# Lambda times alpha1 as one row, spread by one product; lambda itself broadcast by a load

## The chip, the cores and the metric

The kernel runs on one core of a Trainium2 chip. The metric is the device time of one execution in microseconds (us). The core has five engines that the profile names: PE (matrix products; PEld are its weight loads, which overlap PE), DVE (vector work), ACT (activations and copies), POOL (GpSimd) and SP (it issues transfers). Transfers run on 16 DMA engines that all queues share. In this kernel SP and ACT issue the plain ones (queues q1 and q10 of the profile) and POOL those that also change the type (q0).

## What is computed

Attention over keys and values that are averaged in groups of 8, for 8 batches of 8 heads, 576 positions and width 64; then, on the result x (8 x 576 x 512), a residual block that mixes positions and then channels:

```python
k_p = k.reshape(B, H, Sp, 8, D).mean(axis=3)
v_p = v.reshape(B, H, Sp, 8, D).mean(axis=3)
scores = scale * np.matmul(q, k_p.transpose(0, 1, 3, 2))
...
x = attn_out.transpose(0, 2, 1, 3).reshape(B, S, H * D)
...
a1 = alpha1 * x + beta1
tok = np.einsum('ts,bsd->btd', w_tok, a1)
u = x + lam * tok
a2 = alpha2 * u + beta2
ch = np.maximum(a2 @ w_ch1, 0.0) @ w_ch2
return (u + lam * ch).astype(np.float32)
```

lam, alpha1, beta1, alpha2 and beta2 are vectors of 512. Since lam multiplies each column of tok, lam times alpha1 can be multiplied into x before the mixing, and lam times beta1 becomes one more row of the mixing product.

## The kernel before

Tokens are worked on in 9 blocks of 512. Each batch gives four chunks of 128 tokens (positions 0 to 511), and the last 64 positions of two batches make up a ninth. The program's order is written by hand: the tile framework places buffers and semaphores, but each engine runs its instructions in the order of the text. Batch 0 is written out line by line (L806 to L889). From there on a loop over the blocks (L943) gathers pieces of work with a place number each, sorts them by it and calls them (L1018). The first block's list also holds the attention of batch 1.

**Constants at the start.** The tile vecs (L205) has the vectors of the mixing in rows: row 0 of its partition dimension holds lam in slot 0, beta1 in slot 1, alpha1 in slot 2, and row 64 holds lam and beta1 once more. ACT issues the loads of lam (L210, called at L213), of two of the four pieces of the rem tile (L148; the last 64 positions of q and k for batch 0), of alpha1 (L218) and of beta2 (L222). SP issues the other two rem pieces, beta1 and alpha2 as rows of b2row. POOL issues q, k and v with a change of type. Meanwhile DVE fills constants; L276, L278 and L280 build the pooling matrices out of what POOL prepares, and come last before the program proper.

**Lambda and lambda times alpha1 on all 128 partitions.** The tile lam_bc holds lam in every partition, and lamal_bc holds lam times alpha1. spread_lam (L301) makes the first: a product of a row of ones (ones_row, 1 x 128) with the lam row, f32, into the PSUM tile ps_bc, and a copy by ACT (L305). spread_al1 (L307) makes the second in two halves of 256 columns: a product of ones with half of alpha1 (L311), then a product of that with lam_bc on DVE (L312).

**Batch 0.** In order: att_F transposes q (L402), cast_rem converts the rem pieces (L170), att_Frem transposes them (L426), spread_lam comes, then double_k and att_K form the pooled keys (L445, L451) and copy them to kpT (L461, one half on ACT, one on DVE), then spread_al1(0) and bias_row(0) (L284, lam times beta1, on DVE). The heads follow: att_S forms scores (L493, L496) and their exponentials (L498, ACT), first_V the pooled values (L472, L474, copy L477), att_AV the attention products (L556, L560) and the division (L562, L564, DVE). att_X (L578) and rest_X (L571) multiply x by lamal_bc into xs: heads 0 to 3 read columns 0 to 255, heads 4 to 7 the others. spread_al1(1) stands between the scores of head 6 and the attention product of head 5. load_al2 (L297) broadcasts alpha2 to all partitions by a load on SP, behind a DVE memset that sets the moment of its issue. keep_warm products on PE stand in gaps. setup_wtok transposes w_tok (L329). mix_T is the mixing product (L614) with the sum on DVE (L618) and, for batch 0, a product with al2_bc (L624).

**Who reads lam_bc later.** scale_w2 (L721) multiplies w2 by lam, from place 13.9 of the first block's list on; mlp_B (L688) multiplies the output of the first block by lam. After that w2 itself carries lam. setup_wtok_odd (place 8.3 of the first block) copies a part of wtT by two loads on SP (L347, L348), the second behind a DVE memset (L346). load_v32 loads batch 1's values on POOL's queue, and sum_v (L137) is the first to read them.

The lines that the change takes out or moves most:

```python
load_vector(0, moe_lam)
load_rem(0)
...
nc.scalar.dma_start(out=vecs[0:1, 2], in_=moe_alpha1.unsqueeze(0))
...
spread_lam()
double_k(0)
att_K(0, 0, None)
spread_al1(0)
...
att_S(0, 6)
spread_al1(1)
att_AV(0, 5)
```

Of the kernel before, what the change touches and what calls it, by code (L numbers as in the profile page):

```python
# [11 lines left out]
ALU = mybir.AluOpType  # L12
AX = mybir.AxisListType

P = 128
SPG = 72
DM = 512
# [6 lines left out]
def kernel(  # L24
# [18 lines left out]
    nc = tc.nc  # L43
# [8 lines left out]
    def gp(name):  # L52
        return psA.tile([P, 512], FP, tag="gp", name=name)
# [13 lines left out]
    def new_batch(b):  # L67
        st1[b] = {"qT": [None] * 2, "ET": [None] * H, "raw": [None] * 2, "q": [None] * 2,
                  "k": [None] * 2, "v": [None] * 2}
# [4 lines left out]
    def load_q_bf(b, u, behind=None):  # L74

        bf = work.tile([P, 4, 4, D], BF, tag="q_bf", bufs=4, name="q_bf")
        if behind is not None:
            behind.memset(bf[:, 0, 0, 0:1], 0.0)
        nc.gpsimd.dma_start(out=bf.rearrange("p h c d -> p h (c d)"), in_=rows(q, b, u))
        st1[b]["q"][u] = bf  # L80
# [60 lines left out]
    def load_rem(b, queue=nc.sync, behind=None):  # L141

        raw = work.tile([P, 2, 2, 2, D], FP, tag="rem_raw", bufs=2, name="rem_raw")
        if behind is not None:
            behind.memset(raw[:, :, :, 0, 0:1], 0.0)
        for i, src in enumerate((q, k)):
            for h in range(2):
                (nc.scalar if h and not b else queue).dma_start(  # L148
                    out=raw[:, i, h].rearrange("p c d -> p (c d)"),
                    in_=src[b, h::2, 512:576, :].rearrange("a (i c) d -> i a (c d)", c=2))  # L150
        st1[b]["rem_raw"] = raw
# [48 lines left out]
    lam_bc = const.tile([P, DM], FP, tag="lam_bc", name="lam_bc")  # L200
    lamal_bc = const.tile([P, DM], FP, tag="lamal_bc", name="lamal_bc")
# [3 lines left out]
    vecs = const.tile([65, 3, DM], FP, tag="vecs", name="vecs")  # L205
    ones_row = const.tile([1, P], FP, tag="ones_row", name="ones_row")
    nc.vector.memset(ones_row, 1.0)

    def load_vector(i, src, queue=nc.scalar):
        queue.dma_start(out=vecs[0:65:64, i], in_=src.unsqueeze(0).to_broadcast((2, DM)))  # L210

    new_batch(0)
    load_vector(0, moe_lam)  # L213
    load_rem(0)
    load_q_bf(0, 0)
    load_k16(0, 0)
    load_vector(1, moe_beta1, nc.sync)
    nc.scalar.dma_start(out=vecs[0:1, 2], in_=moe_alpha1.unsqueeze(0))  # L218
    start = const.tile([1, 2], FP, tag="start", name="start")
    nc.vector.memset(start, 0.0)  # L220
    nc.scalar.activation(out=start[:, 1:2], in_=start[:, 0:1], func=AF.Exp, bias=0.0, scale=1.0)
# [45 lines left out]
    for i in range(2):  # L267
# [5 lines left out]
    nc.vector.memset(pool_v[:, 64:], 0.0)  # L273
    nc.vector.memset(pool_vr, 0.0)
    nc.vector.memset(vr16, 0.0)
    nc.vector.tensor_scalar(out=pool_v[:, 0:64], in0=pool_main, scalar1=8.0, scalar2=None,  # L276
                            op0=ALU.mult)
    nc.vector.tensor_tensor(out=pool_vr[0:32, 64:72], in0=pool_v[0:32, 0:16:2],  # L278
                            in1=pool_v[0:32, 1:16:2], op=ALU.add)
    nc.vector.tensor_reduce(out=pool_rem, in_=pool_each, op=ALU.max, axis=AX.X)  # L280

    def bias_row(i):
        p0 = 64 - 64 * i
        nc.vector.tensor_tensor(out=xs_pool[i][p0:p0 + 1, 4, :], in0=vecs[p0:p0 + 1, 1],  # L284
                                in1=vecs[p0:p0 + 1, 0], op=ALU.mult)
# [12 lines left out]
        behind.memset(al2_bc[:, 0:1], 0.0)  # L298
        nc.sync.dma_start(out=al2_bc, in_=moe_alpha2.unsqueeze(0).to_broadcast((P, DM)))

    def spread_lam():  # L301

        ps = gp("ps_bc")
        nc.tensor.matmul(out=ps, lhsT=ones_row, rhs=vecs[0:1, 0])
        nc.scalar.copy(out=lam_bc, in_=ps)  # L305

    def spread_al1(half):  # L307

        ps = gp("ps_bc")[:, 0:256]
        cols = slice(256 * half, 256 * half + 256)  # L310
        nc.tensor.matmul(out=ps, lhsT=ones_row, rhs=vecs[0:1, 2, cols])  # L311
        nc.vector.tensor_tensor(out=lamal_bc[:, cols], in0=lam_bc[:, cols], in1=ps, op=ALU.mult)  # L312

    def setup_vectors():
        ps = gp("ps_vec")
# [19 lines left out]
    def setup_rowsum(tcx):  # L335

        trc = P if tcx < 4 else REM
        cols = slice(P * tcx, P * tcx + trc)
        ps = gp("ps_rs")
        for sc in range(5):  # L340
            nc.tensor.matmul(out=ps[:, 0:trc], lhsT=ones_bf if sc < 4 else ones_lo,
                             rhs=wtT[:, sc, cols], start=(sc == 0), stop=(sc == 4))
        nc.scalar.copy(out=wtT[64:65, 4, cols], in_=ps[64:65, 0:trc])
# [35 lines left out]
    def setup_bias(js):  # L379
        ps_bias = gp("ps_bias")  # L380
        for i, jc in enumerate(js):
            for cc in range(4):
                nc.tensor.matmul(out=ps_bias[0:P, i:i + 1], lhsT=w1_of(cc, jc),
                                 rhs=b2c_bf[:, cc:cc + 1], start=(cc == 0), stop=(cc == 3))
        nc.scalar.copy(out=bias_cols[:, js[0]:js[-1] + 1], in_=ps_bias[0:P, 0:len(js)])
# [45 lines left out]
    def double_k(u):  # L431

        nc.vector.tensor_copy(out=st1[0]["k"][u][:, :, 4], in_=st1[0]["k"][u][:, :, 0])
        if u == 0:
            cast_rem_k(nc.vector)

    def att_K(b, u, copy):

        st = st1[b]
        ps_kp = gp("ps_kp")  # L440
        kp = ps_kp[:, 0:4 * SPG].rearrange("p (h g) -> p h g", g=SPG)
        n, nr = (1, 1) if b else (4, 2)
        for h in range(4):
            for c in range(n):
                nc.tensor.matmul(  # L445
                    out=kp[:, h, 0:64],
                    lhsT=st["k"][u][:, h, c:c + 2].rearrange("p a d -> p (a d)"),
                    rhs=pool_main, start=(c == 0), stop=(c == n - 1))
        for hh in range(2):
            for c in range(nr):  # L450
                nc.tensor.matmul(  # L451
                    out=kp[:, hh:4:2, 64:72],
                    lhsT=st["rem"][1][:, hh, c:c + 2].rearrange("p a d -> p (a d)"),
                    rhs=pool_rem.rearrange("p (g u r) -> p u r g", r=2, u=2)[:, u],
                    start=(c == 0), stop=(c == nr - 1))
        if b:
            copy(out=kp_pool[u], in_=kp)
            return
        for a in range(2):
            rows = slice(64 * a, 64 * a + 64)  # L460
            (copy or (nc.scalar.copy, nc.vector.tensor_copy)[a])(  # L461
                out=kpT_pool[u][rows, a], in_=kp[rows])
# [138 lines left out]
    def keep_warm(count):  # L601

        ps = psB.tile([P, DM], FP, tag="ch", bufs=2, name="ps_warm")
        for _ in range(count):
            nc.tensor.matmul(out=ps, lhsT=warm[:, 0:P], rhs=warm)
# [211 lines left out]
    keep_warm(1)  # L817
    att_Frem(0, nc.scalar.copy)
    keep_warm(1)
    spread_lam()  # L820
    double_k(0)
    att_K(0, 0, None)
    spread_al1(0)
    bias_row(0)
    att_S(0, 0)
    att_S(0, 1)
# [18 lines left out]
    att_S(0, 5)  # L845
    att_AV(0, 4)
    att_S(0, 6)
    spread_al1(1)
    att_AV(0, 5)
    att_X(0, 4, 6, nc.gpsimd, False)  # L850
    att_S(0, 7)
# [91 lines left out]
    for n in range(NBLK):  # L943
        todo = []
# [26 lines left out]
        if n >= FIRST:  # L971
# [22 lines left out]
            else:  # L994
                for m in range(4):
                    todo.append((27.2 if m < 2 else 29.2, lambda m=m: store(n, m)))
        if n == 0:
            todo.append((6.2, lambda: setup_rowsum(4)))
            todo.append((8.3, setup_wtok_odd))
            for g in range(2, 4):  # L1000
                todo.append((4 * g - 0.8, lambda g=g: setup_bias(range(4 * g, 4 * g + 4))))
# [48 lines left out]
```

## Time and profile before

| | us |
|---|---|
| median of 3 runs | 333.59 |
| the three runs | 333.06, 333.59, 334.97 |
| the profiled execution | 333.62 |
| its span, first to last instruction | 331.9 |
| PE busy | 323.7 (98% of the span) |
| DVE busy | 233.6 (70%) |
| ACT busy | 175.7 (53%) |
| POOL busy | 95.2 (29%) |

The instructions that the change touches, from the trace's answers for their tiles:

| line | engine | what | count | ns each | start, us |
|---|---|---|---|---|---|
| L304 | PE | ones times lam, 1x512 f32 | 2 | 692 and 587 | 7.7, 8.2 |
| L305 | ACT | copy to lam_bc, 128x512 | 1 | 586 | 8.9 |
| L311 | PE | ones times half of alpha1, 1x256 f32 | 4 | 374 to 478 | 9.8 and 18.4 |
| L312 | DVE | lam_bc times that, 128x256 | 2 | 422 | 10.8, 19.2 |
| L299 | SP | issue of the alpha2 broadcast, 256 KB | 1 | 363 | 17.9 |

An f32 product stands as two passes in the trace, each with its own weight load. Times of matmuls are those of single instructions, which overlap their neighbours; the chain of waits gives what each adds to the path. In a view of the timeline a line reads: start, duration, engine, line of the program, operation, output from input, count, and in brackets how long the engine sat idle before it and what ended that. An engine's name with a q (ACTq, SPq) is the issue of a transfer, not the transfer. In a table by stretches the columns are the stretch, its length, busy time and count for PE, PEld, DVE, ACT and POOL, then the granted TensorE clock as a share of full speed, the mean number of DMA engines' share at work, and GB/s.

### The profile page before, as it was taken

What the parts mean: (1) busy time and instruction counts of PE and PEld (TensorE: products, weight loads), DVE (VectorE), ACT (ScalarE), POOL (GpSimd) and SP (SyncE); (2) the same over time, 40 slices, a digit from 0 to 9 for tenths busy, and PEclk for the clock granted to TensorE, in tenths of its full rate; (3) what the DMA queues carried; (4) which work ended last, traced back from release to release, by engine and by line L of the source; (5) the groups of instructions that cost most, each with busy time, mean ns of one, the idle gap of its engine ahead of it and who ended that gap; (6) DMA issues with size and microseconds to landing.
All of it is one profiled execution on the core that took longest, in us unless ns stands there. A gap on an engine that the chain in (4) does not pass through costs nothing.

```text
span 331.9 us, 6477 instructions
## 1 busy us (share of the span) xinstructions
PE 323.7 (98%) x2500; PEld 209.6 (63%) x2531; DVE 233.6 (70%) x485; ACT 175.7 (53%) x322; POOL 95.2 (29%) x110
## 2 busy tenths in 40 slices
PE   7999999999999999999999999999999999999995
PEld 3667864455544576656775677558755866586584
DVE  6674289989679969676967796877788783263263
ACT  3584989448422861388128812682268225703710
POOL 8669828401247011800280027102510200000000
PEclk9799999999999999999999999999999999999999
DMA  8999999966895992499449943996340044004003
GB/s 117 191 217 270 270 209 245 206 148 101 152 243 99 219 181 81 80 232 173 147 109 209 173 136 73 209 187 176 65 136 2 0 65 143 2 0 127 1 32 97
DMA packets 66472, 45.81 MB, mean 138 GB/s; under 512 B 34397, under 2 KB 57061, under 8 KB 66442
## 3 DMA queue, kind: packets, MB, share of 16 engines
q1 hardware_dynamic: 52092, 32.67, 43.3%
q0 software_dynamic: 13824, 12.40, 22.9%
q8 instruction: 20, 0.33, 0.4%
q10 hardware_dynamic: 526, 0.34, 0.4%
q14 instruction: 10, 0.08, 0.1%
HBM read 38.30 MB, written 9.44 MB: 144 GB/s over the span
## 4 chain that ended last, share of the span: by engine, by line
PE 94%; DMA 2%; DVE 1%; issue 1%; POOL 1%; ACT 0%; POOLq 0%
PE ps_h L662 38%; PE ps_w L785 26%; PE ps_tok L614 11%; PE ps_ch L682 8%; PE ps_av L556 3%; PE ps_s L513 2%; DMA k<-in_k_dram 2%; PE ps_kp L445 1%; PE ps_sc L493 1%; PE ps_r L520 1%; PE ps_av L560 1%; PE ps_v L472 0%; PE ps_w L329 0%; PE ps_q L402 0%; DVE u_sb L618 0%
## 5 line engine op out<-in xcount | busy, mean ns | idle before, releaser
L662 PE MATMUL ps_h<-u_fm,w 128*128 128x512 bf16 (+2 forms) x588 | 132.6, 368 | 1.3 <-DVE bias_cols L665 0.2
L669 ACT ACTIVATE H<-ps_h,bias_cols 128x512 bf16<-128x512 f32 x144 | 98.2, 688 | 56.5 <-PE ps_h L662 55.5
L662 PEld LDWEIGHTS <-w 128*128 128x128 bf16 x608 | 65.6, 114 | 49.9 <-issue 2.2
L785 PEld LDWEIGHTS <-H 128*128 128x128 bf16 x560 | 53.5, 98 | 10.8 <-DVE u_sb L803 1.2
L622 ACT CAST u_bf<-u_sb 128x512 bf16<-128x512 f32 x32 | 19.8, 618 | 69.9 <-issue 39.9
L785 PE MATMUL ps_w<-w_l,H 128*128 128x256 bf16 x448 | 53.6, 272 | 0.0
L803 DVE TENSOR_TENSOR u_sb<-u_sb,ps_w 128x512 f32<-128x512 f32 x54 | 36.3, 683 | 17.1 <-PE ps_w L785 17.1
L578 POOL TENSOR_TENSOR xs<-x_tm,lamal_bc 128x512 bf16<-128x512 f32 x12 | 15.9, 1328 | 108.7 <-DVE x_tm L564 108.5
L614 PE MATMUL ps_tok<-xs,wtT 128*128 128x512 bf16 (+3 forms) x194 | 44.6, 380 | 0.4
L618 DVE TENSOR_TENSOR u_sb<-x_tm,ps_tok 128x512 f32<-128x512 f32 (+1 forms) x40 | 27.4, 684 | 9.9 <-PE ps_tok L614 9.8
L564 DVE TENSOR_TENSOR x_tm<-ps_av,rec 128x320 f32<-128x320 f32 x64 | 31.5, 492 | 2.6
L542 ACT ACTIVATE ET<-ps_s 72x512 f16<-72x512 f32 x56 | 32.3, 592 | 0.0
L614 PEld LDWEIGHTS <-wtT 128*128 128x128 bf16 (+3 forms) x200 | 17.4, 100 | 16.0 <-issue 1.1
L562 DVE RECIPROCAL rec<-ps_av 128x5 f32<-128x5 f32 x64 | 12.2, 190 | 16.9 <-PE ps_av L560 16.7
L483 DVE TENSOR_TENSOR v_u<-v_u 72x1024 f32<-72x1024 f32 (+1 forms) x24 | 22.7, 948 | 0.2
L785 PE MATMUL ps_w<-w_t,h_s 128*128 128x256 bf16 x168 | 22.6, 272 | 0.0
L682 PEld LDWEIGHTS <-H 128*128 128x128 bf16 x128 | 11.9, 98 | 13.7 <-issue 0.4
L754 DVE TENSOR_TENSOR H<-H,H 128x1024 bf16<-128x1024 bf16 x14 | 9.7, 690 | 14.3 <-ACT H L669 14.2
L185 POOL TENSOR_TENSOR k_raw<-k_raw 128x512 f32<-128x512 f32 x14 | 18.8, 1341 | 0.9 <-PE ps_ch L682 0.7
L785 PEld LDWEIGHTS <-h_s 128*128 128x128 bf16 x168 | 16.4, 98 | 4.1
L187 POOL TENSOR_TENSOR k_bf<-k_raw 128x512 bf16<-128x512 f32 x14 | 18.5, 1319 | 1.1
L754 DVE TENSOR_TENSOR h_s<-H 128x1024 bf16<-128x1024 bf16 x21 | 14.4, 686 | 6.0 <-ACT H L669 5.8
(148 smaller groups left out, 367.6 us busy)
## 6 DMA issues: line engine op xcount, KB each, us to landing
out_dram<-u_sb SPq DMA_DIRECT2D x29, 256.0 KB
k_raw<-in_k_dram SPq DMA_DIRECT2D x12, 512.0 KB
v_u<-in_v_dram SPq DMA_DIRECT2D x12, 512.0 KB
q_bf<-in_q_dram POOLq DMA_DIRECT2D x16, 256.0 KB, 7.3
w<-in_moe_w_ch_dram POOLq DMA_DIRECT2D x6, 512.0 KB, 12.5
out_dram<-u_sb SPq DMA_DIRECT2D x11, 128.0 KB
w<-in_moe_w_ch_dram POOLq DMA_DIRECT2D x1, 1024.0 KB, 15.0
k_raw<-in_k_dram POOLq DMA_DIRECT2D x2, 512.0 KB, 16.8
```

What stands on the lines that cost most here:

```text
L483: nc.vector.tensor_tensor(out=out, in0=t[:, :, 0:width], in1=t[:, :, width:2 * width], op=ALU.add)
L542: nc.scalar.activation(out=o, in_=i, func=AF.Exp, bias=0.0, scale=0.125)
L564: nc.vector.tensor_tensor(out=x[:, 1 - odd:6 - odd, dd:dd + D], in0=av[:, :, 0:64], in1=rec.unsqueeze(2).to_broadcast((P, 5, D)), op=ALU.mult)
L614: nc.tensor.matmul(out=ps_tok[p0:p1], lhsT=wtT[0:kk, at, P * c:P * c + p1 - p0], rhs=xs_pool[i][0:kk, sc, :], start=(sc == 0), stop=(sc == 4))
L618: nc.vector.tensor_tensor(out=s["u"][p0:p1, :], in0=x[p0:p1, 1 + c if c < 4 else 5 - 5 * i, :], in1=ps_tok[p0:p1, 0:DM], op=ALU.add)
L622: nc.scalar.copy(out=s["u_bf"], in_=s["u"])
L662: nc.tensor.matmul(out=ps_h[:, t0:t1 + one], lhsT=w1_of(cc, j), rhs=rhs, start=(cc == 0), stop=(cc == 3))
L669: nc.scalar.activation(out=H4[n, j // 4][:, j % 4, :], in_=ps_h, func=AF.Relu, bias=bias_cols[:, j:j + 1], scale=1.0)
L682: nc.tensor.matmul(out=ps, lhsT=H_of(n, j)[:, 128 * m:128 * m + 128], rhs=(w2l if n else w2)[j // 4][:, j % 4, :], start=(j == 0), stop=(j ...
L754: nc.vector.tensor_tensor(out=o, in0=a, in1=b, op=op)
L785: nc.tensor.matmul(out=ps, lhsT=stat(j), rhs=moving(j), stop=(j == 7), start=(first and (pp == 0 or alone) and j == 0), skip_group_check=True)
L803: nc.vector.tensor_tensor(out=o, in0=o, in1=banks[key, "both"], op=ALU.add)
```

## The change

Alpha1's load moves up on ACT, to just behind lam's. On DVE, ahead of L276, a product of the alpha1 row with the lam row overwrites the alpha1 row. One product of ones with that row and one copy by ACT, spread_lamal, give lamal_bc directly, in the place where spread_lam stood. Both calls of spread_al1 go, with the PSUM tile of each. lam_bc is filled by a broadcast load on SP, load_lam, made like load_al2, behind a DVE memset; it stands at place 1.5 of the first block's list, which is the first place of that list.

```diff
     new_batch(0)
     load_vector(0, moe_lam)
+    nc.scalar.dma_start(out=vecs[0:1, 2], in_=moe_alpha1.unsqueeze(0))
     load_rem(0)
     load_q_bf(0, 0)
     load_k16(0, 0)
     load_vector(1, moe_beta1, nc.sync)
-    nc.scalar.dma_start(out=vecs[0:1, 2], in_=moe_alpha1.unsqueeze(0))
...
     nc.vector.memset(vr16, 0.0)
+    nc.vector.tensor_tensor(out=vecs[0:1, 2], in0=vecs[0:1, 2], in1=vecs[0:1, 0], op=ALU.mult)
     nc.vector.tensor_scalar(out=pool_v[:, 0:64], in0=pool_main, scalar1=8.0, scalar2=None,
                             op0=ALU.mult)
...
-    def spread_lam():
+    def spread_lamal():
 
         ps = gp("ps_bc")
-        nc.tensor.matmul(out=ps, lhsT=ones_row, rhs=vecs[0:1, 0])
-        nc.scalar.copy(out=lam_bc, in_=ps)
-
-    def spread_al1(half):
-
-        ps = gp("ps_bc")[:, 0:256]
-        cols = slice(256 * half, 256 * half + 256)
-        nc.tensor.matmul(out=ps, lhsT=ones_row, rhs=vecs[0:1, 2, cols])
-        nc.vector.tensor_tensor(out=lamal_bc[:, cols], in0=lam_bc[:, cols], in1=ps, op=ALU.mult)
+        nc.tensor.matmul(out=ps, lhsT=ones_row, rhs=vecs[0:1, 2])
+        nc.scalar.copy(out=lamal_bc, in_=ps)
+
+    def load_lam(behind):
+        behind.memset(lam_bc[:, 0:1], 0.0)
+        nc.sync.dma_start(out=lam_bc, in_=moe_lam.unsqueeze(0).to_broadcast((P, DM)))
...
-    spread_lam()
+    spread_lamal()
     double_k(0)
     att_K(0, 0, None)
-    spread_al1(0)
     bias_row(0)
...
     att_S(0, 6)
-    spread_al1(1)
     att_AV(0, 5)
...
         if n == 0:
+            todo.append((1.5, lambda: load_lam(nc.vector)))
             todo.append((6.2, lambda: setup_rowsum(4)))
             todo.append((8.3, setup_wtok_odd))
```

## The prediction

> **What bounds the kernel now.** I read the page first, then the chain of waits in order of time, then the timelines of DVE and ACT over the first 20 us, then stretches cut at the changes of the TensorE clock, and last the DMA queues in short stretches.
>
> ```profile
> span 331.9 us, 6477 instructions
> PEclk9799999999999999999999999999999999999999
> PE 94%; DMA 2%; DVE 1%; issue 1%; POOL 1%; ACT 0%; POOLq 0%
> ```
>
> PE holds 94% of the chain. What an edit is worth is therefore the PE time that it takes out of the chain, or the PE wait that it makes. The change touches the first 60 us only, so the chain there is what counts.
>
> ```profile
> 2.25 6.64 DMA k<-in_k_dram
> ...
> 8.93 0.81 PE ps_kp L445 x16
> 9.74 0.10 PE ps_kp L451 x4
> ...
> 9.87 0.40 ACT kpT L461
> ...
> 10.29 0.47 DVE kpT L461
> ...
> 10.81 0.33 PE ps_sc L493
> ...
> 18.50 0.62 PE ps_bc L311 x2
> 19.12 0.23 PE ps_av L556 x4
> ```
>
> The columns are start, time on the chain, and what. Three things are to be seen. Up to 8.9 us everything waits for the load of k, so PE work before that is covered. From 9.84 to 10.81 the chain runs through the two copies of kpT, not through PE, and the first half of the alpha1 product (L311, on PE from 9.76 to 10.45) lies beside them. The second half of that product stands on the chain itself, with 0.62 us.
>
> **The change part by part.** The sum is made against the profiled execution: 333.62 us, of which 331.9 are the span and 1.72 lie around it. The median shown is 333.59, so the same difference holds for it.
>
> *The second half product goes* (PE L311 at 18.43, DVE L312 at 19.16, 0.42 us). PE gets its 0.62 us of the chain back. The exponentials on ACT next show 0.48 us of waiting for PE before 19.53, so ACT can follow by 0.48; the attention products on PE follow in order. What is late next: the chain is PE without a break from there to 25.31, where DVE and POOL take over with work that waits for PE. POOL's first product with alpha2 starts at 24.75 and would start at about 24.1. The alpha2 load was issued at 17.86 behind a memset that doesn't move, so it doesn't get earlier; since no wait for it shows before, all that is known is that it has landed by 24.75, so the gain is cut to anything down to 0 if it lands after 24.1. I take **-0.62** (the load has 6.2 us even then), with 0 as the other end.
>
> *The first half product goes* (PE L311 0.69 us, DVE L312 at 10.79, 0.42 us). PE waits for kpT until 10.81 anyway; DVE has no chain work between 10.75 and 13.16. **0**. The cover is the pair of kpT copies (0.40 and 0.47 us); without it 0.62 more would be gained.
>
> *The one product left* (1 row by 512, then the copy on ACT) is the same as lambda's before: PE 1.12 us from 7.70, ACT 0.59 from 8.85, in the same place. **0**.
>
> *The row product on DVE* is new: 1x512 f32, both inputs in SBUF. The nearest row is the bias row, L284.
>
> ```profile
> 5.59 0.54 DVE L276 TENSOR_SCALAR pool_v<-pool_main 128x64 bf16<-128x64 bf16 x1 [1.03 <-POOL pool_main L248]
> 6.88 0.30 DVE L170 CAST rem_q<-rem_raw 128x256 bf16<-128x256 f32 x1 [0.37 <-DMA rem_raw<-in_q_dram]
> ...
> 11.24 0.68 DVE L284 TENSOR_TENSOR xs<-vecs 1x512 bf16<-1x512 f32 x1
> ```
>
> It costs 0.68 us, and DVE idles 1.03 us just there, from 4.56 to 5.59. It is free if alpha1 has landed by 5.59 - 0.68 = 4.9. Behind it in DVE's order stand L276, L278 and L280 (0.93 us from 5.59 to 6.52), then the cast of rem_q at 6.88, for which PE's transposes, and behind those the broadcast product and the k products, wait. With alpha1 landing at T the cast starts at T + 0.68 + 0.93, which is later than 6.88 by T - 5.27. PE's broadcast product ends at 8.82 and the k products start at 8.93, so 0.11 us of that is covered: the loss is T - 5.38.
>
> When does alpha1 land? Its load (0.52 us of issue, ACT's fourth, at 3.33) becomes ACT's second, at 1.97.
>
> ```profile
> 0.81 1.13 ACTq L210 DMA_DIRECT2D vecs<-in_moe_lam_dram  x1
> 1.97 0.62 ACTq L148 DMA_DIRECT2D rem_raw<-in_q_dram  x1
> 2.62 0.67 ACTq L148 DMA_DIRECT2D rem_raw<-in_k_dram  x1
> 3.33 0.52 ACTq L218 DMA_DIRECT2D vecs<-in_moe_alpha_dram  x1
> ```
>
> Cut into short stretches, the DMA view shows ACT's queue (q10) with 4 packets between 2.30 and 2.50 (lambda's), none from 2.5 to 5.0, and 144 from 5.0 to 6.5, which are the rem load issued at 1.97. So early bound: as lambda, some 0.5 us after the end of the issue, T = 3.0. Late bound for a load in the rem load's place: first packets at 5.06 and up to 0.6 us until the count arrives (alpha1's own packet ran at 7.00, and its count came at 7.68 by the trace's semaphore record), T = 5.7, a loss of 0.32. One packet behind nothing else on its queue is nearer to lambda's row: **0**.
>
> *ACT's two rem loads* are issued 0.52 us later, from 2.49 and 3.14. DVE waits for the first (0.37 us before 6.88). Bounds: 0, since its packets began only at 5.06, 2.5 us after its issue had ended, so that something other than the issue held them; and 0.52 - 0.11 = 0.41 if all of it passes on. I take **+0.1**. ACT's table load and the beta2 load keep their times, since the number of issues ahead of them is the same. SP's queue is untouched here.
>
> *Lambda by a load* at the head of the first block: a DVE memset (0.06 us, as L298) between L665 at 30.77 and L665 at 33.82, in 2.88 us of idle time: 0. Then a 256 KB broadcast on SP, 0.36 us of issue, as alpha2's. On SP it stands ahead of the two wtT copies (issued at 24.09 and 37.60): the first moves to about 31.4, behind the memset, and nothing reads its target before the fifth chunk of batch 1, after 54 us. 0. The load lands like alpha2's within 6.9 us (17.86 to its reader at 24.75), by 38; the first reader of lambda is the scaled w2 at 47.53. 0. But 256 KB at the 239 to 306 GB/s that the queues move from 25 to 40 us is about 1 us of the DMA engines. The tightest of the loads behind it is v_main: issued at 28.69, landing 11.6 us later at 40.29, first read by DVE L137 at 41.42. That leaves 1.13 us, 0.5 once PE is 0.62 ahead. Bounds: 0, and 1.0 - 0.5 = 0.5 as a stall of DVE, of which the 0.22 us that DVE waits for PE before L477 is covered: 0.3. I take **+0.1**.
>
> Sum: -0.62 + 0.1 + 0.1 = **-0.42 us**, 333.62 to **333.2** (from the median the same).
>
> **The clock.** It is a term of its own, since PE at half rate lies on the chain from 10.95.
>
> ```profile
> 7.54:10.95 3.41, 3.18 (x29) 1.52 (x28) 1.48 (x7) 2.05 (x6) 3.09 (x6) 1.00 1.46 185
> 10.95:14.37 3.42, 3.42 (x22) 2.29 (x22) 1.79 (x6) 1.92 (x7) 1.85 (x3) 0.50 1.32 190
> ```
>
> Second column PE busy, third from the right the granted clock. In the stretch from 7.54 PE was busy for 3.18 of 3.41 us, and the clock still fell to half for the next 3.42. So it wasn't idleness that cost the clock; 1.8 us of that busy time is the f32 products of one row, of which the change takes 0.69 out. I take no change: the stretch loses work that evidently didn't hold the clock.
>
> The Trainium skill, "TensorE: Matmul & The Clock Gate", Part 1, says that the gate follows how busy PE was over windows of 3413 ns and opens after a busy one. The window's length agrees with the 3.41 us here; the rule that busy PE keeps the clock does not. By that rule the change speaks against itself: it empties the stretch further, and one more window at half rate would add 3.41 / 2 = 1.7 us, a time of 334.9; by the row it adds nothing.
>
> **The rivals.**
>
> *The gain is absorbed* (333.6). The alpha2 load, which doesn't move, or v_main ends what follows. For it: both have slack of the gain's own size. Against: neither shows as a wait before. 0.15.
>
> *The clock stays up* (331.7). With 0.69 us less of one-row f32 work the stretch ahead isn't judged empty, and the half-rate window vanishes. PE does in its 3.42 us what takes 1.7 at full rate; ACT's exponentials bound it to about 1.2 (four heads at 1.55 us a pair: 3.1 from 10.72, 13.8 instead of 15.06). 333.2 - 1.2 to 1.7 = 331.5 to 332.0. Against: nothing full-width is added. For: the three runs before lie 1.9 us apart, about one such window. 0.2.
>
> *The row product stalls DVE* (slower, 335.0). Alpha1's packet, in spite of its earlier issue, is served only after the rem loads, as in the run before: T = 7.1 to 7.7. Loss T - 5.38 = 1.7 to 2.3, less 0.42 (the term for the rem loads stays in) = 1.3 to 1.9 over 333.62: 334.9 to 335.5. It decides from T = 5.8 on, where the loss eats the 0.42. For: a gap from 2.5 to 5.0 without a packet on that queue. Against: lambda's load, first on the same queue, ran within 0.4 us of its issue. 0.15.
>
> That the change doesn't do what it says (lambda's load late for its reader) would need 16 us for 256 KB; alpha2's took under 6.9.
>
> **How the numbers follow.** Forecast 0.5, the rivals 0.15, 0.2 and 0.15. A measurement of this kernel tells about 0.5% from no change, 1.67 us: below 331.92 and above 335.26. Forecast and absorbed gain are within, 0.65. Of the clock's 0.2 three quarters lie beyond, 0.15, and runs that differ by a window in the forecast add 0.04: faster 0.19. Of the stall's 0.15 about half lies beyond, 0.08, and runs with one half-rate window more add 0.05: slower 0.13. The rest, 0.68, is same. The range holds the forecast with its bounds (-0.62 to +0.2), and most of the clock case and of the stall: 331.7 to 334.9.
>
> **What would show it.** Right: no ps_bc on the chain at 18.5, the AV product after it 0.5 to 0.6 us earlier; the row product on DVE before 5.6 and the rem_q cast within 0.2 of 6.88; the chain still passing k's load at 8.9; the clock low for one window near 11; the memset of lam_bc near 30.4 and no DMA wait on DVE near 41. Wrong: DVE waiting for alpha1 after 5, the k products on PE starting after 9.1, a half-rate window more or less, POOL waiting for alpha2 at 24.

## The result, and the profile after

The changed kernel takes 335.06 us (median of 22 executions, 332.71 to 337.24) against 333.50 us (22 executions, 331.94 to 335.60): a ratio of 1.0048, with an interval of 1.0030 to 1.0066. It is slower by 0.48%, where 333.2 us was forecast. The profiled execution took 335.95 us, 334.1 of them in its span.

The page of the changed kernel: the span, the granted TensorE clock in 40 slices, and the chain's shares by engine.

```profile
span 334.1 us, 6471 instructions
...
PEclk9979999999999999999999999999999999999999
...
PE 91%; DMA 3%; POOL 2%; issue 1%; DVE 1%; POOLq 0%
```

The dip of the clock has moved from the second slice (8 to 17 us) to the third (17 to 25 us), and PE has lost three points of the chain to DMA and POOL. The chain of the changed kernel, in order of time (start, time on the chain, what), shows where:

```profile
7.05 0.74 POOL q_bf L79
7.79 0.72 POOL v L113
8.51 11.13 DMA wt_bf<-in_moe_w_tok_dram
...
19.69 0.47 PE ps_w L327 x5
```

The second half product is off the chain, as forecast. But the chain no longer passes k's load at 8.9 us, where the forecast still had it: it goes through the load of w_tok, which POOL issues at 8.51 and for which PE now waits. PE's timeline of before and then of the changed kernel at that point:

```profile
19.44 0.24 PE L496 MATMUL ps_sc<-rem_qT,kpT 128*72 128x64 bf16 x1
19.52 0.45 PE L329 MATMUL ps_w<-identity_bf,wt_bf 128*128 128x128 bf16 x5
```

```profile
17.68 0.39 PE L491 MATMUL ps_sc<-qT,kpT 128*72 128x256 bf16 x2
17.90 0.24 PE L494 MATMUL ps_sc<-rem_qT,kpT 128*72 128x64 bf16 x1
19.69 0.47 PE L327 MATMUL ps_w<-identity_bf,wt_bf 128*128 128x128 bf16 x5 [1.55 <-DMA wt_bf<-in_moe_w_tok_dram]
```

PE comes to the last of the scores 1.5 us earlier than in the profile of before (17.90 against 19.44; there PE had run at half rate from 10.95 to 14.37), waits 1.55 us, and starts on w_tok at 19.69 against 19.52. In before there was no such wait: by the trace's semaphore record w_tok had landed at 18.15, 1.37 us before PE came to it; in the changed kernel it landed at 19.64. Then the clock falls. The changed kernel in stretches cut at its clock changes (stretch, length, busy time and count of PE, PEld, DVE, ACT and POOL, granted clock, DMA share, GB/s):

```profile
6.43:13.26 6.83, 5.60 (x56) 3.17 (x55) 3.58 (x14) 4.22 (x11) 5.47 (x8) 1.00 1.40 186
13.26:16.68 3.42, 3.42 (x62) 2.81 (x61) 3.02 (x11) 2.97 (x8) 2.75 (x3) 1.00 1.11 207
16.68:20.09 3.41, 1.76 (x27) 1.28 (x26) 1.58 (x6) 2.02 (x7) 3.21 (x5) 1.00 1.12 211
20.09:23.50 3.41, 3.41 (x32) 2.58 (x30) 2.04 (x7) 1.64 (x3) 1.14 (x2) 0.50 1.20 235
```

In the stretch with the wait PE is busy for 1.76 of 3.41 us, and the next 3.41 us run at half rate. In these two profiles PE is 0.17 us behind the kernel before at 19.5 us, 1.83 us behind at 23.5, and stays 1.83 behind to its last matmul. So nearly all of their difference arose in the first 24 us; the last 0.4 us of the span's difference (2.24 us) arise at the end, in the last stores (below). Both profiles hold one stretch of 3.41 us at half rate, each in another place.

The clock differs from execution to execution of one and the same kernel. Here an execution has *lost the clock* if its mean granted clock is below 0.9965 (one half-rate stretch of 3.41 us gives 0.995, two give 0.988 or 0.989), and all others are at *full clock*. Over the four series of the experiments below the kernel before lost it in 43 of 130 executions; for its 22 executions beside the result no clock is on record. At full clock those series' medians are 332.7 to 332.8 us, with the clock lost 334.5 to 335.1, so a loss is worth about 2 us. The changed kernel lost it in 16 of 22, and its six at full clock have a median of 333.62 (332.71 to 335.24). So, as an estimate across series, there are two terms: 0.40 more executions out of one (16/22 less 43/130) times 2 us is 0.8, and 0.8 to 0.9 us come on top at full clock. The second rests on six executions that lie far apart; e4, e5, e8 and f1 below, which hold the same change, have 333.0 to 333.8 us at full clock.

### The profile page after: what moved, and what is told of

It reads as the page before. It is cut to its first block, busy times and chain, and to the rows that moved or that the text cites. A ratio compares the mean times of both kernels' runs of the same rounds, so it can differ in the third digit from the quotient of the medians.

```text
span 334.1 us, 6471 instructions
## 1 busy us (share of the span) xinstructions
PE 323.8 (97%) x2496; PEld 209.6 (63%) x2527; DVE 233.2 (70%) x485; ACT 175.8 (53%) x322; POOL 95.5 (29%) x110
## 4 chain that ended last, share of the span: by engine, by line
PE 91%; DMA 3%; POOL 2%; issue 1%; DVE 1%; POOLq 0%
PE ps_h L660 37%; PE ps_w L783 26%; PE ps_tok L612 11%; PE ps_ch L680 8%; DMA wt_bf<-in_moe_w_tok_dram 3%; PE ps_s L511 2%; PE ps_av L554 2%; PE ps_w L327 1%; PE ps_r L518 1%; PE ps_av L558 1%; PE ps_kp L443 1%; POOL v L113 0%; DVE u_sb L616 0%; POOL k L85 0%; PE ps_warm L603 0%
```

## The experiments

Each kernel was timed against the kernel before in one series on one chip: e1 to e4, e5 to e8, f1 to f4 and g1 to g3, on three chips in all (the f and g series on the same one). The ratio is that on record, estimated over the executions; it is not the quotient of the two medians, which for e2 would be 1.006. "Dummy matmul" is one product of keep_warm, 128x512, whose result nobody reads.

| kernel | median, us | ratio [95%] | clock lost | median at full clock |
|---|---|---|---|---|
| before, four series | 333.06 to 333.32 | | 43 of 130 | 332.68 to 332.81 |
| changed | 335.06 | 1.0048 [1.0030, 1.0066] | 16 of 22 | 333.62 |
| e1 lambda's load alone | 332.87 | 0.9980 [0.9958, 1.0001] | 1 of 12 | 332.76 |
| e2 early part alone | 335.21 | 1.0028 [1.0001, 1.0056] | 8 of 12 | 332.97 |
| e3 half products out alone | 333.05 | 0.9992 [0.9969, 1.0015] | 3 of 12 | 332.86 |
| e4 changed, half products back | 333.44 | 1.0016 [0.9990, 1.0042] | 3 of 12 | 333.25 |
| e5 changed, PE busy before w_tok | 335.05 | 1.0035 [1.0010, 1.0059] | 7 of 12 | 333.57 |
| e6 alpha1's load moved alone | 335.27 | 1.0033 [1.0000, 1.0066] | 7 of 12 | 332.77 |
| e7 row product alone | 332.78 | 0.9999 [0.9976, 1.0022] | 3 of 12 | 332.76 |
| e8 changed, alpha1 on SP | 333.94 | 1.0022 [1.0001, 1.0043] | 4 of 12 | 333.76 |
| f1 changed, filled | 333.26 | 0.9988 [0.9964, 1.0012] | 1 of 12 | 333.02 |
| f2 alpha1 on SP, w_tok earlier, filled | 335.41 | 1.0047 [1.0018, 1.0075] | 8 of 12 | 334.00 |
| f3 changed, w_tok earlier | 335.68 | 1.0076 [1.0037, 1.0114] | 6 of 8 | 334.41 |
| f4 row product late | 333.62 | 1.0002 [0.9975, 1.0029] | 2 of 12 | 333.55 |
| g1 before, filled | 332.78 | 0.9990 [0.9963, 1.0016] | 2 of 12 | 332.62 |
| g2 alpha1 moved, filled | 333.22 | 0.9998 [0.9970, 1.0026] | 2 of 12 | 333.07 |
| g3 before, emptied | 333.27 | 1.0008 [0.9981, 1.0036] | 5 of 12 | 332.34 |

### First series: the parts of the change

**e1**, the load of lambda alone, in the kernel before:

```diff
+    def load_lam(behind):
+        behind.memset(lam_bc[:, 0:1], 0.0)
+        nc.sync.dma_start(out=lam_bc, in_=moe_lam.unsqueeze(0).to_broadcast((P, DM)))
...
+            todo.append((1.5, lambda: load_lam(nc.vector)))
```

> The kernel before, with the 256 KB load of lambda added at the head of the first block (it writes the same values over lam_bc). Theory A (the early part: the row product on DVE stretches POOL's work beside it by 0.2 us and the rem loads are issued 0.5 us later, so that the w_tok load is late): no change, ratio 1.000. Theory B (the products taken from PE: PE arrives at w_tok before it has landed, waits, and the clock falls): 1.000. Theory C (the load of lambda takes DMA time that something waits for): all of the loss, 1.005.

**e2**, the early part alone: the load of alpha1 moved, and the row product into a row of its own.

```diff
     load_vector(0, moe_lam)
+    nc.scalar.dma_start(out=vecs[0:1, 2], in_=moe_alpha1.unsqueeze(0))
...
-    nc.scalar.dma_start(out=vecs[0:1, 2], in_=moe_alpha1.unsqueeze(0))
...
+    row = const.tile([1, DM], FP, tag="row", name="row")
+    nc.vector.tensor_tensor(out=row, in0=vecs[0:1, 2], in1=vecs[0:1, 0], op=ALU.mult)
```

> The kernel before, with alpha1's load moved up on ACT and the row product added on DVE ahead of pool_v; its result goes to a row of its own that nobody reads. Theory A: all of the loss, 1.005, with POOL's select of identity at 0.50 instead of 0.31 us, the rem_q cast at about 7.4 and w_tok landing later than 18.5. Theory B: 1.000 to 1.001 (0.35 us from the rem loads at most). Theory C: 1.000.

**e3**, the half products out alone:

```diff
     def spread_al1(half):
-        ps = gp("ps_bc")[:, 0:256]
         cols = slice(256 * half, 256 * half + 256)
-        nc.tensor.matmul(out=ps, lhsT=ones_row, rhs=vecs[0:1, 2, cols])
-        nc.vector.tensor_tensor(out=lamal_bc[:, cols], in0=lam_bc[:, cols], in1=ps, op=ALU.mult)
+        nc.vector.tensor_copy(out=lamal_bc[:, cols], in_=lam_bc[:, cols])
```

> The kernel before, without the two half products of ones with alpha1; DVE copies lambda into lamal_bc in their places, so that alpha1 is left out of what is computed. Theory A: faster by the 0.6 us of the chain or equal, 0.998 to 1.000. Theory B: the loss, 1.003 to 1.005, with PE waiting for w_tok and the clock at half in the stage after it. Theory C: 0.998 to 1.000.

**e4**, the changed kernel with the two half products back on PE, where they stood:

```diff
+    def half_product(half):
+        ps = gp("ps_bc")[:, 0:256]
+        nc.tensor.matmul(out=ps, lhsT=ones_row, rhs=vecs[0:1, 2, 256 * half:256 * half + 256])
...
     att_K(0, 0, None)
+    half_product(0)
...
     att_S(0, 6)
+    half_product(1)
```

> The changed kernel, with the two half products of ones put back on PE in their places; nobody reads them. Theory A: no better than the changed kernel, 1.005 or more (0.6 us more on the chain would make 1.006). Theory B: as the kernel before, 1.000 to 1.001. Theory C: 1.005.

Measured: e1 costs nothing (0.9980), so the load of lambda is out. e2 costs 1.0028 and loses the clock in 8 of 12. e3 gains nothing in the median (0.9992), though its profiled execution started on w_tok at 17.75 us, 1.8 before the profile of before, which had a stretch at half rate ahead of it. e4 (1.0016, 3 of 12) can't be told from before, as theory B had it; but theory B's other half, that e3 would be slow, did not come. The early part, which had been priced at +0.1, costs time by itself.

### Second series: the early part taken apart

**e5**, the changed kernel with three dummy matmuls in the wait for w_tok:

```diff
+    keep_warm(3)
     setup_wtok(0, nc.scalar.copy)
```

> The changed kernel, with three full-width warm products (0.22 us each) on PE ahead of the w_tok transposes, as many microseconds as the second half product took there. Theory G (PE, with less to do, stands before w_tok, the stretch is judged empty and more executions lose the clock for one or two windows of 3.41 us): fewer executions with a mean clock below 0.997 than the 16 of 22 of the changed kernel, and 1.000 to 1.002. Theories P and R (the early part is what costs): as the changed kernel or 0.6 us more, 1.005 to 1.007.

**e6**, the kernel before with alpha1's load second on ACT:

```diff
     load_vector(0, moe_lam)
+    nc.scalar.dma_start(out=vecs[0:1, 2], in_=moe_alpha1.unsqueeze(0))
     load_rem(0)
...
-    nc.scalar.dma_start(out=vecs[0:1, 2], in_=moe_alpha1.unsqueeze(0))
```

> The kernel before, with only alpha1's load moved up to second on ACT, so that the two rem loads there are issued 0.3 to 0.5 us later. Theory R (the rem loads: PE's transposes of them start later, PE stands still longer in the first 10 us, and more executions lose the clock): ratio 1.003 to 1.005 and more than half of the executions below a mean clock of 0.997. Theory P (the row product on DVE stretches POOL's select beside it from 0.31 to 0.50 us, all later loads of POOL are issued 0.2 us later, w_tok among them): 1.000. Theory G: 1.000.

**e7**, the kernel before with a row product at the place of the change, of rows that have landed in time anyway:

```diff
     nc.vector.memset(vr16, 0.0)
+    row = const.tile([1, DM], FP, tag="row", name="row")
+    nc.vector.tensor_tensor(out=row, in0=vecs[0:1, 0], in1=vecs[0:1, 0], op=ALU.mult)
```

> The kernel before, with only a row product of the same shape added on DVE in the same place (lambda by lambda, into a row that nobody reads); no load is moved. Theory P: POOL's select at 0.50 us, the w_tok load issued at 8.5 instead of 8.3, ratio 1.003 to 1.005. Theory R: 1.000. Theory G: 1.000.

**e8**, the changed kernel with alpha1 loaded by SP, so that ACT's rem loads keep their places:

```diff
-    nc.scalar.dma_start(out=vecs[0:1, 2], in_=moe_alpha1.unsqueeze(0))
+    nc.sync.dma_start(out=vecs[0:1, 2], in_=moe_alpha1.unsqueeze(0))
     load_rem(0)
```

> The changed kernel, with alpha1's load issued by SP ahead of its rem loads instead of by ACT ahead of its own; ACT's rem loads go out as in the kernel before. Theory R: as the kernel before or 0.6 us faster, 0.998 to 1.001. Theory P and theory G: as the changed kernel, 1.004 to 1.006.

Measured: e6, which moves one load of 2 KB and nothing else, costs 1.0033 (its interval just reaches 1.0000) and loses the clock in 7 of 12, where the kernel before lost it in 7 of 35 on that chip; at full clock it is the kernel before (332.77 us). e7 costs nothing. e8 keeps the clock better than the changed kernel (4 of 12), but not its time at full clock (333.76). e5 cures nothing: dummy matmuls ahead of w_tok are not enough (its profiled execution had lost the clock at 11.67 us, long before them). DVE's timeline of e6, where the cast of q's remainder starts:

```profile
7.83 0.60 DVE L170 CAST rem_q<-rem_raw 128x256 bf16<-128x256 f32 x1 [1.33 <-DMA rem_raw<-in_q_dram]
```

and e6 in stretches cut at its clock changes:

```profile
5.66:12.49 6.83, 5.52 (x49) 3.00 (x48) 3.75 (x14) 3.19 (x8) 6.23 (x10) 1.00 1.45 201
12.49:19.32 6.83, 6.83 (x68) 5.13 (x66) 4.02 (x12) 4.05 (x12) 3.04 (x4) 0.50 1.15 212
```

The cast starts 0.95 us later than before's (6.88), though its load's issue moved by 0.3 us only (2.27 against 1.97); PE waits 0.84 us for it, is busy for 5.52 of 6.83 us, and the next 6.83 us run at half rate. The moment of the cast varies by itself (6.88, 7.88, 7.08 and 7.84 in before, e1, e3 and e7, which leave ACT's order alone; 7.42, 7.24, 7.63, 7.58 and 7.83 in the five with the load moved), so single profiles can't price the move. The counts can: the five kernels with the load moved (changed, e2, e4, e5, e6) lost the clock in 16 + 8 + 3 + 7 + 7 = 41 of 70 executions, and in the two series of e1 to e8 those without it (21 of 70 of the kernel before, and 1, 3, 3 and 4 of 12 in e1, e3, e7 and e8) in 32 of 118. e4 with its 3 of 12 is the exception. It differs from the changed kernel only by the two half products on PE, so with the load moved these may help to keep the clock; against that, e2 and e6 keep them too and lost it in 15 of 24. The runs don't settle this.

### Third series: fill, w_tok's place, another place for the row product

**f1**, the changed kernel with three dummy matmuls in waits of PE that its profile shows at 7.5 and 10.2 us:

```diff
-    keep_warm(1)
+    keep_warm(2)
     att_Frem(0, nc.scalar.copy)
...
     att_K(0, 0, None)
+    keep_warm(2)
     bias_row(0)
```

> The changed kernel with one more dummy matmul ahead of the products of the first remainder of q (where the tensor engine waited 0.46 us in the changed kernel's profile) and two more behind the first pooled k (0.48 + 0.20 us of waits). If the clock is lost because the first stretch after it opens holds too little full-width work (in the profiles that lost it 3.6 to 4.0 us of other than one-row f32 products in 6.83 us, in those that kept it 4.4 or more), then fewer executions lose it than the changed kernel's 16 of 22: at most 4 of 12, and a median of 333.5 to 334.2 us (ratio 1.001 to 1.003). If it is the wait for w_tok alone, in the second stretch, the time stays at 334.5 to 335.5 us (1.004 to 1.007).

**f2**, f1 with alpha1 on SP as in e8 and w_tok's loads earlier as in f3.

> The changed kernel with alpha1's row loaded by SP, w_tok's first load issued ahead of the last part of v, and the three dummy matmuls in the first waits of the tensor engine. If the three things found so far (remainder loads late, w_tok late, an emptier first stretch) make up the loss, nothing of it is left and the forecast's gain shows: 332.2 to 332.8 us, ratio 0.997 to 0.999, at most 3 of 12 executions with a lower clock. If something else holds it, 333.5 us or more.

**f3**, the changed kernel with w_tok's loads ahead of the last part of v on POOL:

```diff
-    load_v16(0, (2,))
     load_wtok()
+    load_v16(0, (2,))
```

> The changed kernel with w_tok's loads issued ahead of the last part of v. If the wait of the tensor engine for w_tok (1.55 us in the changed kernel, 1.06 us with alpha1 on SP) is what eats the gain of the products, executions at full clock fall from 333.6 to 332.7 us or below, and where that wait is also what loses the clock the median falls to 333.0 us (ratio 0.9995). If the clock is lost earlier, for the loads of the remainders, the median stays at 334.4 to 335.2 us with more than half of the executions at the lower clock.

**f4**, the changed kernel with alpha1's load in its old place, the row product in DVE's idle time at 8 us, four dummy matmuls where the row was spread, and the spreading behind the pooled keys:

```diff
...
     load_vector(1, moe_beta1, nc.sync)
+    nc.scalar.dma_start(out=vecs[0:1, 2], in_=moe_alpha1.unsqueeze(0))
...
     more_constants()
+    nc.vector.tensor_tensor(out=vecs[0:1, 2], in0=vecs[0:1, 2], in1=vecs[0:1, 0], op=ALU.mult)
...
-    spread_lamal()
+    keep_warm(4)
     double_k(0)
     att_K(0, 0, None)
+    spread_lamal()
```

> The changed kernel with alpha1's load back behind the remainders, the row product behind the fills of ones on the vector engine (idle there from 7.92 to 8.90 us in the kernel before), four dummy matmuls where the row was spread, and the spreading behind the first pooled k. Neither the remainders' loads nor the pool select is touched. If these two were the loss: 332.6 to 333.2 us, ratio 0.998 to 1.0, and at most 4 of 12 executions with a lower clock; the spreading then costs about 0.4 us on the path (1.05 us less the 0.68 us of waits there) against 0.62 us of the second half product. If the gap before w_tok is the cause, 334 us or more.

Measured: f1 takes the whole loss away. The clock is lost in 1 of 12 executions, where the changed kernel in its own series lost it in 16 of 22, and the time is 333.26 us, 0.9988 of before. f3 and f2 are misses: moving w_tok up makes another load late. PE's timeline of f2, and then of f3:

```profile
17.25 0.63 PE L470 MATMUL ps_v<-v,pool_v 128*72 128x256 f16 x4 [2.25 <-DMA v<-in_v_dram]
```

```profile
17.55 0.63 PE L470 MATMUL ps_v<-v,pool_v 128*72 128x256 f16 x4 [1.46 <-DMA v<-in_v_dram]
```

The wait has only gone from w_tok to v and is about as long (1.46 us) or longer (2.25), and most executions lose the clock, with the fill (f2, 8 of 12) or without it. In the changed kernel's stretch with the wait, the DMA column above reads 1.12, so on average each of the sixteen engines had a packet under way; that this is why what is moved up makes something else late is likely, but not shown. PE's timeline of f4, in which neither ACT's nor POOL's early order is touched, shows w_tok late too:

```profile
19.73 0.47 PE L326 MATMUL ps_w<-identity_bf,wt_bf 128*128 128x128 bf16 x5 [0.99 <-DMA wt_bf<-in_moe_w_tok_dram]
```

f4 keeps the clock (10 of 12) and is no faster than before (1.0002): its w_tok landed at 19.68, with the issue at 8.29 (8.31 in before). Its four dummy matmuls, in the place where the row was spread, are fill as well, so f4 doesn't show that the order alone keeps the clock.

The one execution of f1 that lost the clock happens to be the profiled one (clock 0.995). Its stretches:

```profile
6.53:13.36 6.83, 6.31 (x60) 3.37 (x59) 3.69 (x13) 4.32 (x11) 5.36 (x8) 1.00 1.32 175
13.36:20.18 6.82, 5.37 (x88) 4.13 (x86) 4.56 (x15) 4.99 (x15) 5.98 (x7) 1.00 1.13 212
20.18:23.60 3.42, 3.42 (x30) 2.75 (x28) 2.46 (x8) 1.87 (x4) 1.13 (x2) 0.50 1.17 235
```

The first 6.83 us, now with 6.31 busy, keep the clock; the second, with a wait of 1.35 us for w_tok in it, loses it, just as in the changed kernel's profile.

### Fourth series: the fill without the change

**g1**, the kernel before with fill:

```diff
-    keep_warm(1)
+    keep_warm(2)
     att_Frem(0, nc.scalar.copy)
...
     spread_al1(0)
+    keep_warm(1)
```

> The kernel before with one more dummy matmul ahead of the products of q's first remainder and one behind alpha1's first half product. If the clock hangs on the work of the first stretch after it opens, then this kernel too loses it less often (at most 2 of 12 executions, where the kernel before lost it in 13 of 31 on the chip of the last runs) and stands at 332.8 to 333.2 us: the 332.8 us of its executions at full clock and up to 0.43 us for two matmuls, ratio 0.998 to 1.0. The changed kernel with its fill (333.26 us) would then be 0 to 0.4 us slower than this, which is what the change costs without the clock. If the fill does nothing to the clock, about 4 of 12 lose it and the ratio is 1.0 to 1.001.

**g2**, e6 with the same fill.

> The kernel before with alpha1's load second on ACT (which alone cost 1.0033 and lost the clock in 7 of 12 executions) and the two dummy matmuls. If the moved load costs time only through the clock, its cost is gone: at most 2 of 12 at the lower clock, 332.8 to 333.2 us, ratio 0.998 to 1.0. If the later remainders cost time by themselves, 333.3 to 333.7 us at full clock; if the clock goes by something else that the moved load does, 6 or more of 12 lose it and the median is 334.5 to 335.3 us.

**g3**, the kernel before without the two dummy matmuls around att_Frem:

```diff
-    keep_warm(1)
     att_Frem(0, nc.scalar.copy)
-    keep_warm(1)
```

> The kernel before without the two dummy matmuls around the products of q's first remainder, nothing else changed: the other direction. They lie in a stretch in which the tensor engine goes on to wait for k, so that they cost no time. If work in the first stretch sets the clock, 7 or more of 12 executions lose it, and the median is 334.5 to 335.3 us, ratio 1.003 to 1.006; if not, 332.6 to 333.3 us with about 4 of 12.

Measured: with fill the moved load's cost is no longer seen (g2, 0.9998, 2 of 12, where e6 had 7 of 12). With it the kernel before loses the clock in 2 of 12. The opposite, g3, is not decisive: 5 of 12, against 9 of 29 of the kernel before on the same chip; 7 had been expected. And g1's profile, one of its two executions without the clock, speaks against the simple reading that only the busy time of the first 6.83 us counts:

```profile
4.16:10.99 6.83, 6.29 (x53) 3.30 (x52) 4.04 (x18) 4.07 (x9) 6.76 (x13) 1.00 1.34 182
10.99:17.82 6.83, 6.83 (x69) 5.29 (x67) 4.18 (x12) 4.12 (x12) 3.64 (x5) 0.50 1.20 199
```

6.29 us busy, and the clock falls; in e6 it fell after 5.52, in f1 it stayed after 6.31 and in g2 after 6.62. What is counted remains open. One thing that the seventeen profiles show is that the moment at which the full clock set in matters. In five it came by 5.0 us after the start, and four of these lost it again 6.83 us later (before 4.13, g1 4.16, e5 4.84, e7 5.00; not e8, 4.71). Of the twelve in which it came later only e6 (5.66) did. So what fill does in a single execution depends on chance too: in g1 the two half-rate stretches followed an early moment, in f1 and g2 the full clock came at 6.53 and 6.25. Only the counts tell that fill keeps the clock more often, where no longer wait is brought in beside it: 5 of 36 lost in f1, g1 and g2 together, against 16 of 22, 43 of 130 and 7 of 12 in the same kernels without fill, partly from other series. Most of this is f1; 2 of 12 in g1 and in g2, taken singly, could be chance. f2, with the fill and a wait of 2.25 us, lost it in 8 of 12.

f1 and g1 are the two kernels with the clock nearly evened out: 0.9988 and 0.9990 of before. With the clock kept, no gain of the change can be measured: f1's median lies 0.5 us above g1's (333.26 against 332.78), in two series whose medians of before differ by 0.23 us the same way. The fastest, g1, can't be told from before either.

## Why the prediction was wrong

**The step that failed is the clock: "I take no change: the stretch loses work that evidently didn't hold the clock."** It rested on one row of one execution: PE busy for 3.18 of 3.41 us, and half rate after it. The runs show a full clock that sets in at another moment in each execution (4.13 to 7.33 us after the start in seventeen profiles) and is lost more often or less with what PE does after that. PE's waits after its full clock has set in, in the profile of before and then of the changed kernel:

```profile
6.60 0.62 PE L402 MATMUL ps_q<-identity_bf,q_bf 128*128 128x128 bf16 x8 [0.90 <-DMA q_bf<-in_q_dram]
```

```profile
7.97 0.29 PE L424 MATMUL ps_qr<-identity_bf,rem_q 128*128 128x128 bf16 x2 [0.46 <-DVE rem_q L170]
...
10.67 0.30 PE L491 MATMUL ps_sc<-qT,kpT 128*72 128x256 bf16 x1 [0.48 <-ACT kpT L459]
11.16 0.30 PE L491 MATMUL ps_sc<-qT,kpT 128*72 128x256 bf16 x1 [0.20 <-DVE kpT L459]
```

Before has besides only waits of about 0.1 us; the changed kernel also has the 1.55 us for w_tok. The waits for q's remainder and for w_tok are not in before's profile, and that for kpT has grown where the first half product went. Taking out the half products does not do it alone: e3 lost the clock in 3 of 12. The moved load alone lost it in 7 of 12, against 7 of 35 of before on the same chip. Which part each has when both come together stays open (e4, above). The loss of the clock rose from 43 of 130 executions to 16 of 22, which makes about 0.8 us of the 1.56 us. By the row nothing was to come. The reading of the Trainium skill's page "TensorE: Matmul & The Clock Gate", Part 1, which the prediction weighed and set aside, had the sign right, though it laid the emptier stretch to the products taken out and not to later loads. The page also says that the window runs free of the kernel's start, with which the moving moment of opening agrees. It gives one idle window as what closes the gate; that is not what the runs show: the clock fell after stretches of 6.83 us with 5.5 (e6) and 6.3 us (g1) of PE work, and stayed after one with 5.6 (the changed kernel's first).

**The rem loads, "+0.1", were mis-sized**, since only the path was priced (bounds 0 to 0.41), not what the wait in it does to the clock. Alone (e6) the moved load cost 1.0033 (1.0000 to 1.0066), about 1.1 us, and nothing at full clock (332.77 us); with fill no cost was seen (g2, 0.9998). ACT's timeline of the changed kernel has the issues:

```profile
1.98 0.27 ACTq L214 DMA_DIRECT2D vecs<-in_moe_alpha_dram  x1
2.29 0.62 ACTq L148 DMA_DIRECT2D rem_raw<-in_q_dram  x1
```

The issue is 0.3 us later than the one of before (1.97), as alpha1's took 0.27 us here and not 0.52; the cast is 0.54 us later.

**The second half product, "-0.62"**: its other end, 0, came true, by another load than the one named. It is off the chain, but at the end of batch 0's scores PE runs into w_tok, which landed between 16.8 and 19.7 us in the fifteen profiles with its issue at 8.3 to 8.6. The prediction went by the waits that before shows, and w_tok showed none, having landed 1.37 us early. By the trace's semaphore record 15 of its 16 counts had come by 17.32 in the changed kernel and the last at 19.64; in before it was 17.44 and 18.15. The end of the kernel follows the start of w_tok's transposes. In the profiles whose clock was full after them, the last DVE addition starts 308.7 to 309.8 us after it (e3: 17.75 and 326.83; f4: 19.73 and 328.61; e6, with half rate ahead of it: 21.67 and 330.41). In the three with half rate after them (changed, f1, f2) it is 309.7 to 310.4. So removed work can count only if w_tok lands early. It did in e3's profiled execution, which didn't wait and took 332.48 us; yet e3's median at full clock (332.86) is not below before's (332.69 in its series). In the profiles of the changed kernel, e8, f1 and f4 PE waited 0.99 to 1.55 us. That goes with their medians at full clock, 333.62, 333.76, 333.02 and 333.55 us, none below before's. Two things stay open: why the last count of w_tok comes late (f4 has POOL's moments of before, and it was late there too), and whether the whole 0.8 to 0.9 us of the changed kernel's six executions at full clock is this wait, since they have no profile. The size would fit: a start at 19.6 to 19.7 us (changed, f1, f4) is 0.4 to 1.6 us later than in the profiles at full clock that keep both half products and did not wait (e1 19.20, g2 18.54, e2 18.30, g3 18.11).

**The row product, 0, was right.** DVE's timeline of the changed kernel:

```profile
4.48 0.62 DVE L276 TENSOR_TENSOR vecs<-vecs 1x512 f32<-1x512 f32 x1
5.80 0.54 DVE L277 TENSOR_SCALAR pool_v<-pool_main 128x64 bf16<-128x64 bf16 x1 [0.70 <-POOL pool_main L248]
...
6.45 0.27 DVE L281 TENSOR_REDUCE pool_rem<-pool_each 128x32 bf16<-128x128 bf16 x1
7.42 0.49 DVE L170 CAST rem_q<-rem_raw 128x256 bf16<-128x256 f32 x1 [0.70 <-DMA rem_raw<-in_q_dram]
```

Alpha1 had landed by 3.5 us (estimated 3.0), the product ran in DVE's idle time, and the cast waited for its own load, not for DVE. The rival that saw DVE stalled is out; e7 alone costs nothing.

**The first half product and the one left, 0 and 0,** stand as far as the path goes: kpT's copies end the wait in the changed kernel too (PE waits 0.48 and 0.20 us for them). **The load of lambda, +0.1**, is at most that: the memset stands at 32.72, the page puts 0.2 us of PE's waiting in the whole kernel down to it, and e1 was not slower than before (0.9980).

**The rivals.** "The gain is absorbed" is what f1 and f4 show, at 0.9988 and 1.0002. "The clock stays up" named the mechanism that makes about half of the loss, with the wrong sign, and for a cause (fewer one-row products) that e3 doesn't bear out: 3 of 12, about as the kernel before.

## What to carry to other kernels

Look at the spread of the runs before a profile: steps of about 2 us between executions of one kernel were the clock, and a change early in a kernel moves how often they come. Waits of PE in the first 20 us had here a price of their own beside the path, and dummy matmuls in waits that are there anyway were a cheap cure (1.0048 of before without them, 0.9988 with them in f1). Before work is taken off PE, look for the load that PE meets next, and how far its landing varies: here it varied by 2.9 us from profile to profile, more than all that was to be gained.

## What was not expected of the hardware

A product of two one-row operands on DVE slows a select on POOL. POOL's timeline of before, and then of the changed kernel:

```profile
4.75 0.31 POOL L243 TENSOR_SCALAR_AFFINE_SELECT identity<-identity 128x128 f32<-128x128 f32 x1
...
8.31 0.57 POOL L194 DMA_DIRECT2D wt_bf<-in_moe_w_tok_dram  x1
```

```profile
4.75 0.50 POOL L243 TENSOR_SCALAR_AFFINE_SELECT identity<-identity 128x128 f32<-128x128 f32 x1
...
8.51 0.57 POOL L194 DMA_DIRECT2D wt_bf<-in_moe_w_tok_dram  x1
```

0.50 or 0.51 us instead of 0.31 in all kernels that have the row product there, 0.31 in those without it and in f4, where it comes later; every load that POOL issues afterwards is 0.2 us later. The Trainium skill's page "SBUF — State Buffer", "Who interferes with whom", has it: DVE and POOL share a pair of ports, and a DVE instruction with two inputs in SBUF reads the second one through the shared read port, against a POOL instruction that reads SBUF. By itself the 0.2 us cost nothing (e7).

The end of the kernel moved too. SP's timeline of the changed kernel, its last two issues:

```profile
329.86 0.55 SPq L700 DMA_DIRECT2D out_dram<-u_sb  x1
330.50 0.54 SPq L696 DMA_DIRECT2D out_dram<-u_sb  x1
```

The last store is issued 0.41 us after the start of the last addition (330.09), where in before it was issued at 328.21 beside an addition at 328.26. The same is seen in e8 (0.66 us) and a little of it in e3 (0.14). In these three a pair of earlier stores together took 1.30 to 1.82 us to issue, against 1.11 in before; in the other profiles the last store is less than 0.1 us behind. The cause is open.
